# Retention, then a two-layer MLP, on one core: four plain fp32 units in place of eight, blocks 0 to 3 in another order, and two pairs at once in batch 1

## The chip, the cores and the metric

The kernel runs on one core of a Trainium2 chip. The time is in microseconds on the device, the median of five runs; a profile of one execution stands beside it. A core has five engines that each work through a queue of instructions in order: PE (TensorE, matmul; its weight loads are shown apart as PEld), DVE (VectorE), ACT (ScalarE), POOL (GpSimd) and SP (SyncE, which here only issues DMAs). Semaphores tie them together. DMAs issued by SP and by ACT run on the same 16 DMA engines. SBUF is the working memory, PSUM the eight banks that matmuls write to.

## What is computed

```python
# q, k, v: (8, 8, 576, 64)  batch, head, position, dim
scores = q @ k.T / sqrt(64)
ret = (scores * Dmat[h]) @ v         # Dmat[h][i, j] = gamma[h] ** (i - j) for i >= j, else 0
x = ret.transpose(0, 2, 1, 3).reshape(4608, 512)
h = x @ w_in                         # (4608, 512) @ (512, 2048)
g = max(h, 0) + alpha * min(h, 0)
out = g @ w_out                      # (4608, 2048) @ (2048, 512), float32
```

The weights arrive as float64 and are turned into float32 on the chip.

## The kernel before

**Blocks, units, cells.** The 4608 rows of x are cut into 18 blocks of 256 tokens, the 2048 hidden columns into 8 units of 256. A cell is one unit of one block: first matmuls (x block times two 128-column strips of w_in), activation, second matmuls into accumulators. A list `order` (lines 869 to 874) says in which order blocks are visited and which units each visit does; a visit that does not finish a block stores its partial sum to memory (`o_kept`) and a later visit of that block loads it again and adds (`has`). Units 0 to 3 are done for all blocks first, because only four units' weights fit in SBUF (`wsl`, slots s, i for unit s and piece i); units 4 to 7 follow, and their weights are loaded back from `w32`, where they were kept after conversion. There are 144 cells.

**Plain and split.** A split cell (`unit`, line 1004, and `second`, line 1053) works in a faster number format with three matmuls per product: x, the weights and g are each cut into three words by ACT, POOL and DVE (`split_x` L906 to L925, `split_w` L677 to L683, `split_g` L1028 to L1037). A plain cell (`unit_plain` L940, `second_plain` L970) uses float32 matmuls on unsplit x and weights and needs no split. The first eight cells are plain: block 0 with units 0 and 1, block 1 with units 0 to 3, block 0 with units 2 and 3. Then blocks 2 to 13 follow with units 0 to 3 each, and so on. A split cell's second matmuls come two cells later (`LAG`).

**Weights.** Each unit has four pieces of 128 x 512 words. `weights(n)` converts the next n pieces: `convert` loads the float64 words (a "raw", 512 KB) into some free room, and ACT (L629, L631), DVE (L639, L641, L650) and POOL (L653) make float32 of it in a "home". The 16 pieces of units 0 to 3 are converted in the opening, with homes in lx0, lx1 and g0, g1, which are free then; the raws go through lx1, w0x and op. DVE's steps use PSUM bank psa1 as a scratch. `split_w(i)` cuts a converted piece into its slot w. The other 16 pieces are converted during the first pass, one each three cells from cell 10 (`ahead`).

**Attention.** Batch 0 is done in three parts (`part_*`, `last_part`; rooms in the weight slots that are still empty) with all heads together. Batches 1 to 7 go by pairs of heads, numbered 4 to 31: `load_kq` and `load_v` load, `operands(n)` scales q on POOL (L719), transposes k and q on DVE (L726) and scales k on ACT (L731); `joint(n)` issues the value matmuls of pair n - 1 (L747) and the score and state matmuls of pair n (L785, L793, L802), then masks the scores into `at` and chains the states through `su` (ACT L844, L854; DVE L849, L857, L860), whose result goes by DMA into `vn` for the value matmuls. kx, qx, at and su exist once, kT, qT, kn and vn twice. The scores and states of every pair use banks psa0 and psa1, the values psh0 and psh1, which the first matmuls of cells use too. For pairs 4 to 7 (`FIRST`) the q and kn loads are issued by ACT and the masks done by ACT and POOL (L816, L822); for the others by SP and DVE (L831). `joint_(x)` does a joint, the operands of the next pair and the loads of the one after. Block 2 needs the values of pairs 4 to 7 and so do blocks 3 and 4 (in part); blocks 0 and 1 need batch 0.

**Order.** The program is written as a list of operations (`do`, `dma`) with engine, assumed cost, what they read and write. `plan()` (line 224) then places them on the engines by list scheduling: at each step the operation that can start first goes next, ties by a due time. The due time comes from PE's own order in the list: each PE operation is wanted at the sum of the costs of those before it, and every other operation is due early enough for its users. The instructions are issued in the order that comes out. `dma` (line 218) issues a load or store on SP or ACT with no limit on how many are under way. Lines 1109 to 1176 list the opening, lines 1178 to 1224 the main loop from cell 8; `todo` says at which cell each later joint comes.

## Time and profile before

| what | value |
|---|---|
| median of 5 runs | 986.21 us (982.54 to 991.15) |
| profiled execution, time | 986.21 us |
| profiled execution, span from first to last instruction | 984.2 us |
| mean granted clock of PE | 0.981 |
| PE busy | 942.4 us, 96% of the span |
| PEld busy | 826.1 us |
| DVE, ACT, POOL busy | 614.7, 583.3, 636.5 us |
| moved by DMA | 134.93 MB, 137 GB/s on average |
| L1004, first matmuls of split cells | 3264 matmuls, 420.2 us |
| L1053, second matmuls of split cells | 1632 matmuls, 403.1 us |
| L940 and L970, plain cells | 128 and 64 matmuls |

The span is cut into 40 slices in the profile; a digit there is a share of a slice in tenths. Busy time of PE is from modelled ends of pipelined matmuls, so a full PE can still lose a little. The granted clock is that of TensorE: where it is 0.5, matmuls take twice as long. A wait in the trace is put down to what released it last.

### The profile page before, as it was taken

The page shows a single profiled execution, that of the slowest core. Times are in us where ns is not written, and L with a number is a line of the kernel's source. Part 1 is how long each engine was busy: PE and PEld are TensorE (multiplying, and loading weights), DVE is VectorE, ACT ScalarE, POOL GpSimd, SP SyncE. Part 2 cuts the span into 40 slices and gives each one's busy share as a digit, 9 for nine tenths or more (in the row PEclk, how much of TensorE's full clock was granted, in tenths as well). Part 3 has the DMA queues.
Part 4 walks back from the last instruction along what each step waited for, and adds up shares of the span by engine and source line. Part 5 has one row for each costly group of instructions (what it writes and reads, how often), then busy time and mean ns, then how long its engine had stood idle before and what let it go on. Part 6 is the DMA issues. An engine that isn't in the chain of part 4 may idle for free.

```text
span 984.2 us, 22760 instructions
## 1 busy us (share of the span) xinstructions
PE 942.4 (96%) x8713; PEld 826.1 (84%) x8713; DVE 614.7 (62%) x1294; ACT 583.2 (59%) x1313; POOL 636.5 (65%) x515
## 2 busy tenths in 40 slices
PE   5897989999999999999999999999999999999998
PEld 4664668889889888887889899999999999999996
DVE  6667766777667787776566777564454444544444
ACT  4464456757556657574686766665555555555542
POOL 4667665767766758574697999665556556565553
PEclk9798889999999999999999999999999999999999
DMA  9988788788675888787442544242212222221111
GB/s 231 225 176 192 157 209 166 183 180 200 172 149 140 196 174 209 162 217 171 164 141 98 176 135 162 79 156 88 65 65 77 79 81 65 66 82 47 43 45 64
DMA packets 255052, 134.93 MB, mean 137 GB/s; under 512 B 218448, under 2 KB 218464, under 8 KB 254944
## 3 DMA queue, kind: packets, MB, share of 16 engines
q1 hardware_dynamic: 238624, 130.59, 51.7%
q10 hardware_dynamic: 16320, 2.89, 1.8%
q8 instruction: 68, 1.11, 0.5%
q14 instruction: 40, 0.33, 0.1%
HBM read 82.19 MB, written 35.65 MB: 120 GB/s over the span
## 4 chain that ended last, share of the span: by engine, by line
PE 84%; DVE 4%; DMA 4%; SPq 3%; ACT 2%; issue 2%; POOL 1%; ACTq 0%; POOLq 0%; DVEq 0%
PE psh L1004 36%; PE pso L1053 34%; PE psh L940 4%; PE psh L747 3%; SPq L220 3%; PE pso L970 3%; PE psa L793 1%; PE psa L802 1%; DMA w<-in_q_dram 1%; DMA vn<-su 1%; DMA kn<-in_k_dram 1%; DVE at L831 1%; PE psh L785 1%; DMA op<-in_moe_w_out_dram 0%; DMA qx<-in_q_dram 0%
## 5 line engine op out<-in xcount | busy, mean ns | idle before, releaser
L1004 PEld LDWEIGHTS psh<-lx,w 128*128 128x128 f32 x3264 | 411.6, 192 | 15.0 <-DVE ga L1019 2.6
L1004 PE MATMUL psh<-lx,w 128*128 128x256 f32 x3264 | 420.2, 285 | 2.0 <-DVE ga L1019 1.2
L1053 PE MATMUL pso<-w,g 128*128 128x512 f32 x1632 | 403.1, 394 | 0.8 <-POOL g L1035 0.3
L1053 PEld LDWEIGHTS pso<-w,g 128*128 128x128 f32 x1632 | 297.2, 189 | 58.2 <-POOL g L1035 1.2
L1032 POOL TENSOR_TENSOR g<-ga,g 128x512 fp32r<-128x512 f32 x136 | 179.1, 1317 | 253.0 <-ACT g L1028 252.6
L1013 DVE SCALAR_TENSOR_TENSOR ga<-psh,gt 128x256 f32<-128x256 f32 x272 | 114.6, 422 | 184.7 <-ACT gt L1012 175.9
L1035 POOL TENSOR_TENSOR g<-g 128x512 fp32r<-128x512 f32 x136 | 177.3, 1303 | 11.7 <-ACT g L1030 1.4
L1019 DVE SCALAR_TENSOR_TENSOR ga<-psh,malpha,ga 128x256 f32<-128x256 f32 x272 | 130.8, 481 | 69.3 <-ACT psh L1016 67.5
L1016 ACT ACTIVATE psh<-ga 128x256 f32<-128x256 f32 x272 | 105.3, 388 | 92.0 <-DVE ga L1013 91.2
L1028 ACT ACTIVATE g<-ga 128x512 fp32r<-128x512 f32 x136 | 85.9, 631 | 117.3 <-PE pso L1053 98.5
L1012 ACT COPY gt<-psh 128x256 f32<-128x256 f32 x272 | 100.9, 371 | 61.4 <-PE psh L1004 53.1
L923 POOL TENSOR_TENSOR lx<-lx 128x512 fp32r<-128x512 f32 x78 | 100.8, 1307 | 17.5 <-DVE lx L913 16.6
L1030 ACT ACTIVATE g<-ga 128x512 fp32r<-128x512 f32 x136 | 84.4, 621 | 0.0
L831 DVE SCALAR_TENSOR_TENSOR at<-psa,pf,mask 64x256 f32<-64x256 f32 x96 | 46.4, 483 | 17.5 <-PE psh L747 9.5
L906 ACT ACTIVATE lx<-x 128x512 fp32r<-128x512 f32 x78 | 47.1, 627 | 0.0
L719 POOL TENSOR_TENSOR qx<-qx,tabx 128x576 f32<-128x576 f32 x28 | 32.5, 1162 | 21.2 <-DMA qx<-in_q_dram 19.9
L747 PEld LDWEIGHTS psh<-at,vn 128*64 128x64 f32 x1008 | 33.0, 138 | 12.9 <-issue 7.2
L920 POOL TENSOR_TENSOR lx<-x,lx 128x512 fp32r<-128x512 f32 x30 | 38.2, 1292 | 3.5 <-ACT lx L918 3.4
L747 PE MATMUL psh<-at,vn 128*64 128x64 f32 x1008 | 38.4, 226 | 2.2 <-DVE ga L1019 1.6
L1071 DVE TENSOR_TENSOR op<-pso,op 128x512 f32<-128x512 f32 x46 | 31.5, 685 | 13.6 <-PE pso L1053 13.6
L940 PE MATMUL psh<-x,lx 128*128 128x256 f32 x96 | 30.0, 477 | 5.8 <-POOL lx L653 2.4
L731 ACT ACTIVATE kn<-kn,tabk 128x576 f32<-128x576 f32 x28 | 21.8, 777 | 22.1 <-DMA kn<-in_k_dram 19.2
(173 smaller groups left out, 863.2 us busy)
## 6 DMA issues: line engine op xcount, KB each, us to landing
ok<-o SPq DMA_DIRECT2D x48, 256.0 KB, 3.1
op<-ok SPq DMA_DIRECT2D x24, 512.0 KB, 4.0
x<-xk SPq DMA_DIRECT2D x23, 512.0 KB, 3.7
xk<-x SPq DMA_DIRECT2D x18, 512.0 KB, 3.6
out_dram<-o SPq DMA_DIRECT2D x36, 256.0 KB, 2.5
kx<-in_k_dram SPq DMA_DIRECT2D x112, 72.0 KB, 3.3
vn<-in_v_dram SPq DMA_DIRECT2D x56, 144.0 KB, 3.6
at<-qT SPq DMA_DIRECT2D x56, 144.0 KB, 3.2
```

The costliest lines, as they stand in the source:

```text
L747: nc.tensor.matmul(pv[i].get()[half(h2), (j - js[0]) * C:(j - js[0] + 1) * C], vns[n % 2][:, h2, j], mt.get()[:, h2, j], start=True, stop= ...
L923: do("POOL", 1.29, lambda c=c: nc.gpsimd.tensor_tensor(out=piece(to.get()[:, 2, c]), in0=to.get()[:, 0, c], in1=to.get()[:, 1, c], op=ALU. ...
L1004: nc.tensor.matmul(at(b), piece(w[:, l, c0:c0 + P]), piece(x.get()[:, l, cc]), start=(n == 0 and cc == 0), stop=(n > 0 and cc == NCC - 1), ...
L1012: do("ACT", 0.36, lambda t=t, at=at: nc.scalar.copy(t(), at(1)), [(ph, 1)], [(gt, f)])
L1013: do("DVE", 0.42, lambda t=t, g=g, at=at: nc.vector.scalar_tensor_tensor(out=g(), in0=at(0), scalar=ONE, in1=t(), op0=ALU.mult, op1=ALU.su ...
L1016: do("ACT", 0.39, lambda g=g, at=at: nc.scalar.activation(at(1), g(), ACTF.Relu, scale=-1.0), [(ga, f)], [(ph, 1)])
L1019: do("DVE", 0.48, lambda g=g, at=at, fc=fc: nc.vector.scalar_tensor_tensor(out=g(), in0=at(1), scalar=malpha[:, fc:fc + 1], in1=g(), op0=A ...
L1028: do("ACT", 0.64, lambda: nc.scalar.mul(piece(to.get()[:, 2]), ga.get(), BELOW), both, [(to, 2)])
L1030: do("ACT", 0.64, lambda: nc.scalar.mul(piece(to.get()[:, 0]), ga.get(), BELOW * 2.0 ** -12), both, [(to, 0)])
L1032: do("POOL", 1.29, lambda: nc.gpsimd.tensor_tensor(out=piece(to.get()[:, 1]), in0=ga.get(), in1=to.get()[:, 2], op=ALU.subtract), both + [ ...
L1035: do("POOL", 1.29, lambda: nc.gpsimd.tensor_tensor(out=piece(to.get()[:, 2]), in0=to.get()[:, 0], in1=to.get()[:, 1], op=ALU.subtract), [( ...
L1053: nc.tensor.matmul(a[2 * m + b].get(), piece(g.get()[:, l, f, m * P:(m + 1) * P]), piece(w_at[u, 2 + f].get()[:, l]), start=(cell["first"] ...
```

## The change

The opening and the plan are rewritten in these points:

1. **Four plain cells.** Only cells 0 to 3 are plain: blocks 0 and 1, each with units 0 and 1. The main loop starts at cell 4.
2. **Visit order.** Blocks 0 and 1 with units 0 and 1 (plain), block 2 with units 0 and 1, block 3 with units 0 to 3, then blocks 2, 1 and 0 with units 2 and 3, all split. From block 4, which is cell 16 in both kernels, the order is as before. There are 44 visits in place of 42, so two more partial sums are kept and added again. A visit whose block is the same as that of the visit before the last reuses its split x without loading or splitting it (visits 4, 21, 24 and 27).
3. **Two chains in batch 1.** Pairs 5 and 7 (`APART`) have their own kx, qx, at and su, in the room of lx0, and use banks pso2 and pso3 for scores and states. The plain cells' accumulators are pso0 and pso1 at every visit.
4. **Weights.** Pieces 0 to 7 get homes in lx1 and g0, with raws in lx0, x3, x4 and op. Pieces 8 to 15 are converted in the room they were loaded to (w3x, op), with no PSUM bank, and split from there. Eight pieces are split before cell 4; pieces 8 to 15 follow between the joints. The conversions of units 4 to 7 start at cell 18.
5. **Backward pass.** The due times come from a list scheduling of the same operations from the end backwards, all engines counted.
6. **Bytes in flight.** In the first 100 us of the plan a DMA on SP waits for an earlier one, so that no more than 1.31 MB, its own included, are under way.

```diff
     def dma(to, fro, size, r, w, eng="SP"):
-        queue = {"SP": nc.sync, "ACT": nc.scalar}[eng]
-        do(eng, 0.56, lambda: queue.dma_start(to(), fro()), r, w, late=size / RATE)
+        def f():
+            ins = {"SP": nc.sync, "ACT": nc.scalar}[eng].dma_start(to(), fro())
+            if now[0] < LIMITED:
+                ahead = size
+                for other, n in reversed(flight):
+                    if eng == "SP" and ahead >= IN_FLIGHT:
+                        tc.add_manual_dep(ins.ins, other.ins.name, mybir.DependencyInfo(
+                            mybir.DependencyClass.Sync, mybir.DependencyReason.DATA),
+                            reason="bytes in flight")
+                        break
+                    ahead += n
+                flight.append((ins, size))
+        do(eng, 0.56, f, r, w, late=size / RATE)
+
+    flight, now = [], [0.0]
+    LIMITED, IN_FLIGHT = 100.0, 5 << 18
...
-            due = [1e9] * len(ops)
-            for op in reversed(ops):
-                due[op.n] = min([want[op.n]] + [due[u.n] - wait(op, u) - op.cost - op.late
-                                                for u in users[op.n]])
...
+        for _ in ops:
+            pick = None
+            for e, queue in ready.items():
+                if queue:
+                    t0 = min(max(free[e], can[op.n]) for op in queue)
+                    op = max((op for op in queue if max(free[e], can[op.n]) <= t0 + 0.02),
+                             key=lambda op: op.n)
+                    t = max(free[e], can[op.n])
                     if pick is None or t < pick[0]:
                         pick = t, op
+            t, op = pick
+            ready[op.eng].remove(op)
+            free[op.eng] = t + op.cost
+            due[op.n] = -(t + op.cost)
+            for d in op.deps:
+                left[d.n] -= 1
+                can[d.n] = max(can[d.n], t + op.cost + wait(d, op) + d.late)
+                if not left[d.n]:
+                    ready[d.eng].append(d)
...
-    LAG, FIRST = 2, range(4, 8)
+    LAG, FIRST, APART = 2, range(4, 8), (5, 7)
...
+    def apart():
+        if not aside:
+            g = Gen(lxs[0])
+            aside.append(g)
+
+            def at(a, b):
+                return lambda: words_of(g)[:, a:b]
+            g.kx, g.qx, mt, su = at(0, S), at(S, 2 * S), at(2 * S, 4 * S), at(4 * S, 4 * S + 8 * D)
...
     def load_kq(n):
         b, c = pairs[n]
-        kx, qx, kn = Gen(kxs), Gen(qxs), Gen(kns[n % 2])
+        if n in APART:
+            kx, qx, kn = apart(), apart(), Gen(kns[n % 2])
+        else:
+            kx, qx, kn = Gen(kxs), Gen(qxs), Gen(kns[n % 2])
...
-        ps = [Gen(psa[p2]) for p2 in range(2)]
+        ps = [Gen(b) for b in ((pso[2], pso[3]) if n in APART else psa)]
...
-    order = [(0, (0, 1)), (1, (0, 1, 2, 3)), (0, (2, 3))]
-    order += [(kb, (0, 1, 2, 3)) for kb in range(2, 14)]
+    order = [(0, (0, 1)), (1, (0, 1)), (2, (0, 1)), (3, (0, 1, 2, 3)), (2, (2, 3)), (1, (2, 3)),
+             (0, (2, 3))]
+    order += [(kb, (0, 1, 2, 3)) for kb in range(4, 14)]
...
     def split_x(vis):
+        if vis["n"] > 3 and visits[vis["n"] - 2]["kb"] == vis["kb"]:
+            vis["x"] = visits[vis["n"] - 2]["x"]
+            return
...
-    raws = iter([((spare, 0), kTs[1]), ((spare, 1024), qTs[1]), ((spare, 2048), was)] +
-                3 * ([((wsl[0, i], 0), None) for i in range(4)] + [((op_, 0), was)]))
+    raws = iter([((spare, 0), kTs[1]), ((spare, 1024), qTs[1]), ((spare, 2048), was),
+                 ((xs[3], 0), kTs[1]), ((xs[4], 0), qTs[1]), ((op_, 0), was), ((xs[3], 0), kTs[1]),
+                 ((xs[4], 0), qTs[1])] + [((wsl[3, i], 0), None) for i in (0, 1, 2, 3, 1, 2, 3)] +
+                [((op_, 0), was)])
...
     part_states(1, bank)
     unit_plain(cells[1])
     load_part(2)
+    load_kq(NPAIR)
+    load_v(NPAIR)
     part_values(1, bank)
     part_carry(1)
     fetch_x(visits[1])
-    load_kq(NPAIR)
-    load_v(NPAIR)
     part_scale(2, 1)
     part_scale(2, 2)
     second_plain(cells[1])
-    unit_plain(cells[2])
     last_part()
     operands(NPAIR)
     load_kq(NPAIR + 1)
     load_v(NPAIR + 1)
-    weights(2)
+    joint_(4)
+    unit_plain(cells[2])
+    joint_(5)
+    for i in range(8):
+        split_w(i)
     second_plain(cells[2])
     unit_plain(cells[3])
...
     joint_(6)
     weights(2)
...
     joint_(7)
-    second_plain(cells[6])
-    unit_plain(cells[7])
+    second_plain(cells[3])
+    weights(2)
     joint_(8)
-    second_plain(cells[7])
-    for i in range(16):
+    for i in range(8, 12):
         split_w(i)
+    for i in range(12, 16):
+        weights(1)
+        if i > 12:
+            split_w(i - 1)
+    split_w(15)
 
-    todo = {}
-    at = 8
-    for b in range(2, B):
-        n = NS * sum(ready_kb[kb] == b - 1 for kb in range(2, 13)) or 6
+    todo = {4: [9], 7: [10], 10: [11], 12: [12]}
+    at = 16
+    for b in range(3, B):
+        n = NS * sum(ready_kb[kb] == b - 1 for kb in range(4, 13)) or 6
...
-    ahead = {10 + 3 * i: 1 for i in range(16)}
+    ahead = {18 + 14 * i // 5: 1 for i in range(16)}
...
-    for cell in cells[8:]:
+    for cell in cells[4:]:
...
     for op in best[1]:
+        now[0] = best[2][op.n]
         op.fn()
```

The lines left out of the diff rename keys and give `load_kq`, `operands`, `values` and `joint` the accessors for the second set of buffers, add the converted-in-place case to `convert`, and put the forward list scheduling, which is otherwise as before, one level out of a loop that ran once.

## The prediction

> **What bounds the kernel now.** I read the page's head and slices first, then the busy time by stage, then the chain of waits, once at the start and once at the end.
>
> ```profile
> span 984.2 us, 22760 instructions
> ...
> PE   5897989999999999999999999999999999999998
> ...
> PEclk9798889999999999999999999999999999999999
> DMA  9988788788675888787442544242212222221111
> ```
>
> A slice is 24.6 us. PE is full from slice 7 to the end, except for one 8 where attention runs out (about 450 to 490 us) and the drain. So time can only come out of the first six slices, out of PE's own work, or out of that one hole. In the early slices the granted clock is down too, and DMA is nearly full.
>
> ```profile
> 0.00:131.50 131.50, 102.28 (x1422) 71.51 (x1422) 93.26 (x195) 67.37 (x130) 82.08 (x85) 0.89 0.90 194
> ```
>
> ```profile
> 82.70:140.10 57.40, 44.51 (x526) 32.13 (x520) 40.87 (x76) 28.63 (x66) 39.52 (x37) 0.82 0.79 174
> ```
>
> The columns are the stretch, its length, busy us of PE, PEld, DVE, ACT and POOL, then granted clock, DMA share and GB/s. Up to the first split cell at 131.5 us PE does something for 102.3 us at a mean clock of 0.89. In the 57.4 us in which batch 1's pairs go through, PE is idle for 12.9 us.
>
> ```profile
> 66.69 0.62 PE psa L793 x32
> ...
> 69.69 3.45 PE psh L940 x16
> ...
> 73.41 3.63 PE pso L970 x8
> ...
> 81.87 0.87 PE psh L747 x24
> 82.76 0.37 ACT x L762
> ...
> 88.51 1.26 POOL g L653
> 89.77 0.04 issue
> 89.81 3.38 PE psh L940 x8
> ...
> 100.38 6.64 PE psh L940 x16
> ...
> 124.12 1.22 PE psh L747 x36
> ...
> 131.53 5.64 PE psh L1004 x24
> ```
>
> Start, length, what. A plain cell costs 3.45 + 3.63 = 7.08 us of PE (L940, L970). After a gap the same 16 matmuls take 6.64 us: half clock. Pair 4's scores (L793) start at 66.69, pair 7's values (L747) at 124.12: 57.4 us for four pairs, one at a time, with gaps of which 82.7 to 89.8 is the longest. The split of block 2 follows, and its first cell starts at 131.53, 6.2 us after those values end.
>
> ```profile
> 962.35 2.87 PE psh L1004 x24
> 965.22 2.75 PE pso L1053 x12
> ```
>
> A split cell costs 2.87 + 2.75 = 5.62 us, 1.46 less than a plain one.
>
> **Where the two kernels meet.** Cell 16, block 4 with unit 0, is the same cell in both, and from it on the same cells and pairs 13 to 31 follow. Before, the 24 L1004 matmuls at 184.98 are the second half of cell 15 and the first of cell 16, so cell 16 starts at 184.98 + 1.43 = 186.4. The change is worth what it moves this point, plus what the other due times do behind it. Before, split cells start at cell 8, at 131.5; after, at cell 4, at a time I call T. From there to cell 16 the kernel before takes 54.9 us for 8 cells and joints 9 to 12; after there are 4 more cells, 4 x 5.62 = 22.5 us. So the move is (T - 131.5) + 22.5 + c, where c is new PE waiting. T = 109 is the break-even.
>
> **T, step by step.** (1) Joint 4 waits for the last part of batch 0, which uses bank psa0 until 64.8. Its transposes run at 58.5, behind the 16 plain matmuls that the chain has at 53.94 to 57.46, though POOL's last scaling of that part (L393) ended at 52.6. The backward pass gives this chain an earlier due time than the plain cell, which is worth those 3.5 us; bounds 0, and 8 from the end of part 1's values (50.3). Joint 4 at 63.2. (2) A pair from scores to values, bare: scores and states 1.09 (0.62 + 0.47, L793 and L802), su copy 0.35, two L849 1.02, copy 0.21, L857 and L860 1.28, the su transfer 2.8, 1.22 of values: 8.0. Pair 4 took 15.2 (66.7 to 81.9), with conversions between its steps. I take 11, nearer the bare chain as half the conversions leave this stretch; bounds 8 and 15. (3) Pairs 5 and 7 get own kx, qx, mt and su and the banks pso2 and pso3, so the four run as two waves: 11 each, 3 for the second pair of the wave (masks on ACT and POOL are 1.9 and 3.1 a pair), and a turn of 4 between (the v load after values takes 3.5 to land, then states 0.47). 11 + 4 + 11 + 3 = 29. Values of pair 7 at 92.2, end at 93.4, and 6.2 for the split: **T = 99.6**, a move of -31.9 + 22.5 = **-9.4**.
>
> **Does DMA allow it?** Needed by T: parts 3.5 MB, twelve pieces 6.3, four pairs at 1.74 each 6.9 (five times 288 KB and 256 of su), loads of pairs 8 and 9 about 2, stores of x and o 2.1: 20.8 MB. At the 194 GB/s of that row it is 107 us, at the 231 of the first 25 us 90. T lies in the middle, so transfers are as much a limit as the chains. The limit of 1.31 MB in flight makes SP wait before issues up to a planned 100 us; behind it on SP all later loads and the at<-qT and vn<-su transfers queue. At 231 GB/s 1.31 MB is 5.7 us of work, and weight transfers already take 5 us to land, so I cost it at nothing; if its waits leave DMA empty for 0.5 us at some ten places it is 5 us.
>
> The Trainium skill, page "DMA: Bandwidth & Descriptors", section "Issuing engines are not separate DMA queues", says that queues share the 16 engines and that using several saves issue time only. By that rule the limit could not shorten the loads on ACT's queue by adding bandwidth; this trace has both queues full together but no row that tests it, and the sum takes no gain here either way.
>
> **c, the crowd in cells 4 to 15.** These 77.4 us now also hold x splits of blocks 1, 0 and 3 and the last pieces. POOL: 12 x 2.62 for g, 4 splits x 5.2, 4 x 1.16 for qx, pieces 12 to 15 at 2.75 (L653 1.34, L678 1.41): 68 us, 88%. DVE: 12 x 1.81, evacuations 11.1 (three visits now add to a kept o), 4 pairs x 6.33, 4 pieces x 2.98 (0.61, 0.55, 0.79 and 1.03 of L639 to L681): 70 us, 90%. Rows of full PE to hold this against:
>
> ```profile
> 200.00:250.00 50.00, 49.88 (x583) 44.89 (x582) 37.25 (x87) 33.78 (x80) 33.29 (x28) 1.00 0.86 202
> ...
> 550.00:600.00 50.00, 49.37 (x319) 44.84 (x318) 34.87 (x63) 33.91 (x76) 47.18 (x36) 1.00 0.49 154
> ```
>
> POOL at 94% left PE 98.7% busy; DVE at 75% cost nothing, and at 90% no full stretch shows it. If DVE can give 81% (20.2 of 25 us from 100 to 125), 70 us need 86, +9. If pieces 8 to 11 are late too, POOL needs 79/0.94 = 84, +6.6. I take **c = +3**, bounds 0 and 9, as POOL's row is the one with PE full. The cover is PE's own work; without it two more splits are 10 us.
>
> **The rest.** Three later visits (21, 24, 27) reuse their x split and one load each goes: POOL and ACT work under a full PE, 0. Two more visits store and reload o, 0 for the same reason. Eight pieces convert in place, where L639 and L641 take 0.61 and 0.55 against 0.69 and 0.70 through a bank: 0.23 each on DVE, off the path. The plain accumulators stay on pso0 and pso1: the next visit waits for two ACT copies of 0.6, long done, 0. The new due times reorder every engine. Behind cell 16 only the hole at 450 to 500 us can answer: 3.7 us idle and 3.4 us at half clock, 5.4 in all. Bounds -5.4 and +5.4; I take **-1.5**.
>
> **Sum:** -9.4 + 3 - 1.5 = -7.9; span 976.3 from 984.2. The profiled execution's time, 986.2, is the median of the runs shown, so the time is **978**.
>
> The clock speaks against fewer plain cells. The trace: 3.2 us lost at 100.4, 2.8 at 131.5, each after a gap. The Trainium skill, page "TensorE: Matmul & The Clock Gate", section "HAM oscillation", says idle gaps above about 3.4 us throw PE to half rate, and its section "What's actually happening" gives 3.4 us to warm up again, a loss of half that, an estimate of 1.7 a gap. Four plain cells cover less, so each of two wave gaps would cost 1.7 by the rule and 3 by the rows; in the sum above only the one ahead of T sits on the path, in 54.9 already.
>
> **Rivals.** (A) The pairs are paced by the engines and the transfers, not by the single buffers: DVE, POOL and DMA were 71, 69 and 79% busy from 82.7 to 140.1, and pairs came every 13 to 15 us. If two chains only interleave, at 12 us a pair with the lighter load, values of pair 7 start at 63.2 + 4 x 12 + 1 = 112, T = 119.6, the sum is +10.6 + 3 - 1.5: time **998**. It decides from T = 109, that is from a mean of some 9.6 us a pair. For it: DMA at 0.9 over this stage. Against: the longest gaps end on one pair's own chain. (B) Gain and crowd cancel: T = 102, c = 7, hole 0: -29.5 + 22.5 + 7 = 0: **986**. For it: DVE at 87%. Against: POOL at 94% with a full PE. (C) The bare chain: 8 us a pair, c = 0: T = 93.6, -15.4 - 1.5: **969**; DMA would need 20.8 MB in 94 us, 222 GB/s, which only the first 50 us exceed (231 and 227).
>
> **Chances.** Forecast 0.46 (own range 972 to 982), C 0.18, B 0.17, A 0.19. Faster by over 0.5% (about what a measurement here can tell from no change, 4.9 us): forecast and C, 0.64; same 0.17; slower 0.19. The range takes C's side down to 962 (with step 1's other end too) and A's up to 995, where pairs come every 11 to 12 us.
>
> **What would show it.** First L1004 matmul near 100 us; L793 groups in two couples; L747 of pair 7 near 92; PE idle under 25 us up to cell 16, near 177; four plain cells (64 L940 matmuls, not 128); no new wait in cells 4 to 15 over 2 us. Wrong, if the first split cell comes after 109, if PE waits on POOL L653/L678 or DVE L681 for unit 2 or 3, or if the stretch behind cell 16 takes other than 798 us by more than 5.

## The result, and the profile after

The kernel after takes 990.07 us (median of 53 runs, 986.35 to 993.91), the kernel before, run beside it, 987.82 us (95 runs, 980.57 to 993.53): a ratio of 1.002, 95% interval 1.0012 to 1.0028. The forecast was 978 and faster; the change costs about 2 us. The profiled executions, 989.2 against 984.2 us of span, lie 5.0 us apart, more than the medians do: that of after was 0.9 us above its kernel's median, that of before 1.6 below. The places below are read from these two.

The page of after, head and slices:

```profile
span 989.2 us, 22943 instructions
...
PE   4786699999999999999999999999999999999997
...
PEclk9998699999999999999999999999999999999999
DMA  9997888777775888778544444243222222221112
```

The hole that the kernel before had at 450 to 490 us is gone, and PE is full from slice 6 on, one slice earlier than before. But slices 4 and 5 now stand at 6, slice 5 at a clock of 0.6: in the opening PE stands more, not less.

The windows view of after: the stretch up to the first split cell, the one up to cell 16, the four pairs, and the old hole (columns as before: stretch, length, busy us of PE, PEld, DVE, ACT, POOL, clock, DMA share, GB/s):

```profile
0.00:112.50 112.50, 74.68 (x1326) 54.97 (x1326) 79.03 (x168) 57.32 (x112) 70.20 (x77) 0.88 0.93 193
112.50:190.40 77.90, 76.22 (x795) 68.24 (x793) 62.27 (x129) 55.01 (x128) 66.85 (x52) 0.97 0.84 204
...
59.50:105.00 45.50, 32.05 (x457) 21.58 (x456) 32.45 (x64) 22.62 (x50) 23.28 (x24) 0.83 0.83 176
450.00:500.00 50.00, 49.50 (x569) 42.90 (x561) 32.68 (x77) 32.83 (x80) 35.72 (x29) 1.00 0.62 178
```

While the four pairs go through (third row) no engine is busy for more than 71% (DVE, 32.45 of 45.5). The DMA engines are at 0.83. It is a stage of waits. In the old hole PE has 49.50 us where the kernel before had 46.26.

PE's timeline in after (start, length, what; in brackets the idle time before and who ended it):

```profile
59.49 0.70 PE L834 MATMUL psa<-qT,kT 64*64 64x64 f32 x32
...
72.52 0.69 PE L834 MATMUL pso<-qT,kT 64*64 64x64 f32 x32 [0.17 <-DVE qT L767]
73.14 0.34 PE L788 MATMUL psh<-at,vn 128*64 128x64 f32 x4
77.19 2.27 PE L788 MATMUL psh<-at,vn 128*64 128x64 f32 x32 [3.71 <-DMA vn<-su]
79.38 5.38 PE L989 MATMUL psh<-x,lx 128*128 128x256 f32 x16
84.69 0.92 PE L788 MATMUL psh<-lx,vn 128*64 128x64 f32 x24
...
88.92 0.70 PE L843 MATMUL psa<-vn,kn 64*64 64x64 f32 x32
...
97.01 2.46 PE L788 MATMUL psh<-at,vn 128*64 128x64 f32 x32 [2.35 <-DMA vn<-su]
...
101.12 0.48 PE L788 MATMUL psh<-lx,vn 128*64 128x64 f32 x4
...
111.42 1.13 PE L834 MATMUL psa<-qT,kT 64*64 64x64 f32 x32 [3.11 <-DVE su L905]
112.48 2.93 PE L1053 MATMUL psh<-lx,w 128*128 128x256 f32 x12
```

L834 are scores (L793 before), L843 states (L802), L788 values (L747), L989 plain first matmuls (L940), L1053 first matmuls of split cells (L1004). Joint 4's scores start at 59.5, values of pair 4 at 73.1 (most of them at 77.2, finished at 79.4), of pair 5 at 84.7, states of pair 6 at 88.9, most of its values at 97.0, pair 7's values at 101.1, the first split cell at 112.5. Before, the same way from joint 4's scores took 57.4 us to pair 7's values; after it takes 41.6, and 29 had been forecast.

The account, by the prediction's own points: T is 112.5, 19.0 earlier. From T to cell 16 it is 77.9 us (190.4 - 112.5), where 54.9 and four more cells make 77.4, so c is +0.5. Behind cell 16 it is 798.8 us against 797.8. That is -19.0 + 22.5 + 0.5 + 1.0 = +5.0.

### The profile page after: what moved, and what is told of

The parts are those of the page before. It is cut to its first block, busy times and chain, and to the rows that moved or that the text cites. A ratio compares the mean times of both kernels' runs of the same rounds, so it can differ in the third digit from the quotient of the medians.

```text
span 989.2 us, 22943 instructions
## 1 busy us (share of the span) xinstructions
PE 937.6 (95%) x8761; PEld 828.9 (84%) x8761; DVE 632.7 (64%) x1306; ACT 589.7 (60%) x1329; POOL 651.3 (66%) x525
## 4 chain that ended last, share of the span: by engine, by line
PE 79%; DMA 8%; DVE 4%; ACT 3%; SPq 2%; issue 2%; POOL 1%; ACTq 0%; POOLq 0%; DVEq 0%
PE psh L1053 37%; PE pso L1102 35%; PE psh L788 3%; SPq L220 2%; DMA kn<-in_k_dram 2%; PE psh L989 1%; PE psa L834 1%; PE psa L843 1%; DMA vn<-su 1%; DMA w<-in_q_dram 1%; DMA w<-in_moe_w_out_dram 1%; DMA lx<-in_q_dram 1%; DMA op<-in_moe_w_out_dram 1%; DMA op<-in_moe_w_in_dram 1%; DMA kx<-in_k_dram 1%
## 5 line engine op out<-in xcount | busy, mean ns | idle before, releaser
L1053 PEld LDWEIGHTS psh<-lx,w 128*128 128x128 f32 x3360 | 423.3, 192 | 21.0 <-DVE ga L1068 8.4
L1053 PE MATMUL psh<-lx,w 128*128 128x256 f32 x3360 | 433.8, 285 | 5.7 <-DVE ga L1068 4.9
L1102 PE MATMUL pso<-w,g 128*128 128x512 f32 x1680 | 413.8, 393 | 0.6 <-POOL g L1084 0.3
L1102 PEld LDWEIGHTS pso<-w,g 128*128 128x128 f32 x1680 | 305.1, 189 | 58.5 <-POOL g L1084 0.7
L1081 POOL TENSOR_TENSOR g<-ga,g 128x512 fp32r<-128x512 f32 x140 | 186.0, 1329 | 226.7 <-ACT g L1077 226.4
L1084 POOL TENSOR_TENSOR g<-g 128x512 fp32r<-128x512 f32 x140 | 183.0, 1307 | 11.3 <-ACT g L1079 0.9
L1068 DVE SCALAR_TENSOR_TENSOR ga<-psh,malpha,ga 128x256 f32<-128x256 f32 x280 | 134.0, 480 | 65.1 <-ACT psh L1065 63.7
L1077 ACT ACTIVATE g<-ga 128x512 fp32r<-128x512 f32 x140 | 88.4, 631 | 121.5 <-PE pso L1102 108.7
L1079 ACT ACTIVATE g<-ga 128x512 fp32r<-128x512 f32 x140 | 86.7, 620 | 0.0
L877 DVE SCALAR_TENSOR_TENSOR at<-psa,pf,mask 64x256 f32<-64x256 f32 x96 | 46.3, 482 | 11.9 <-PE psh L788 3.4
L788 PEld LDWEIGHTS psh<-at,vn 128*64 128x64 f32 x936 | 32.9, 143 | 17.7 <-issue 8.0
L969 POOL TENSOR_TENSOR lx<-x,lx 128x512 fp32r<-128x512 f32 x34 | 44.5, 1308 | 4.8 <-DMA at<-qT 3.4
L788 PE MATMUL psh<-at,vn 128*64 128x64 f32 x936 | 38.4, 232 | 8.8 <-DMA vn<-su 7.2
L1120 DVE TENSOR_TENSOR op<-pso,op 128x512 f32<-128x512 f32 x52 | 35.6, 685 | 14.3 <-PE pso L1102 14.3
L760 POOL TENSOR_TENSOR qx<-qx,tabx 128x576 f32<-128x576 f32 x26 | 30.2, 1162 | 15.0 <-DMA qx<-in_q_dram 11.5
L1125 DVE SCALAR_TENSOR_TENSOR o<-pso,op 128x512 f32<-128x512 f32 x52 | 35.7, 687 | 1.1
L803 ACT COPY x<-psh 128x256 f32<-128x256 f32 (+3 forms) x84 | 23.4, 319 | 20.6 <-PE psh L788 12.7
## 6 DMA issues: line engine op xcount, KB each, us to landing
ok<-o SPq DMA_DIRECT2D x52, 256.0 KB, 3.2
out_dram<-o SPq DMA_DIRECT2D x36, 256.0 KB, 4.1
```

Of the source, the lines that this page charges most:

```text
L788: nc.tensor.matmul(pv[i].get()[half(h2), (j - js[0]) * C:(j - js[0] + 1) * C], vns[n % 2][:, h2, j], mt.mt()[:, h2, j], start=True, stop=True)
L1053: nc.tensor.matmul(at(b), piece(w[:, l, c0:c0 + P]), piece(x.get()[:, l, cc]), start=(n == 0 and cc == 0), stop=(n > 0 and cc == NCC - 1), ...
L1068: do("DVE", 0.48, lambda g=g, at=at, fc=fc: nc.vector.scalar_tensor_tensor(out=g(), in0=at(1), scalar=malpha[:, fc:fc + 1], in1=g(), op0=A ...
L1077: do("ACT", 0.64, lambda: nc.scalar.mul(piece(to.get()[:, 2]), ga.get(), BELOW), both, [(to, 2)])
L1079: do("ACT", 0.64, lambda: nc.scalar.mul(piece(to.get()[:, 0]), ga.get(), BELOW * 2.0 ** -12), both, [(to, 0)])
L1081: do("POOL", 1.29, lambda: nc.gpsimd.tensor_tensor(out=piece(to.get()[:, 1]), in0=ga.get(), in1=to.get()[:, 2], op=ALU.subtract), both + [ ...
```

## The experiments

Fifteen kernels; each ratio is to the kernel before, run beside it. That kernel's own median was between 987.82 and 990.25 us in the several rounds, so compare the ratios and not the medians. "First split cell", "cell 16" and the stretch behind it are from each one's profiled execution, which lies between 2.1 us below (b_kn_sp) and 4.3 us above (a_eight_more) its kernel's median.

How far such readings scatter can be read from five of the kernels. In the traces of after, a_no_limit, a_eight_more, a_eight_big and a_reuse4 every engine has the same instructions in the same order up to the first split cell. It starts at 112.5, 113.0, 113.9, 114.4 and 114.4 us, and cell 16 at 190.3 to 192.3. So a difference of 2 us in these two columns shows nothing by itself, and the stretch behind cell 16 scatters more.

| kernel | median, us | ratio, 95% interval | first split cell | cell 16 | behind it |
|---|---|---|---|---|---|
| before | 987.82 | 1 | 131.5 | 186.4 | 797.8 |
| after | 990.07 | 1.002 (1.0012 to 1.0028) | 112.5 | 190.4 | 798.8 |
| a_no_limit | 989.98 | 1.001 (0.9993 to 1.0026) | 113.0 | 190.3 | 796.9 |
| a_old_due | 1011.67 | 1.0229 (1.0209 to 1.025) | 110.9 | 199.8 | 811.2 |
| a_one_chain | 1000.89 | 1.0114 (1.0093 to 1.0136) | 126.8 | 203.3 | 796.2 |
| a_visits | 992.04 | 1.0032 (1.0012 to 1.0052) | 112.7 | 196.3 | 795.8 |
| a_kn_sp | 987.39 | 0.9989 (0.9974 to 1.0005) | 112.0 | 190.9 | 797.3 |
| a_unit3_early | 986.33 | 0.9976 (0.9961 to 0.9991) | 111.6 | 188.5 | 797.7 |
| a_both | 989.2 | 0.999 (0.9972 to 1.0009) | 115.0 | 192.5 | 798.5 |
| a_eight_more | 992.47 | 1.0024 (1.0006 to 1.0042) | 113.9 | 192.1 | 803.0 |
| a_eight_big | 988.24 | 0.9982 (0.9963 to 1.0001) | 114.4 | 191.7 | 797.2 |
| a_no_unit2 | 985.87 | 0.9957 (0.9942 to 0.9972) | 109.1 | 188.9 | 795.2 |
| a_reuse4 | 988.07 | 0.9984 (0.997 to 0.9997) | 114.4 | 192.3 | 792.7 |
| a_reuse4_unit3 | 981.76 | 0.9927 (0.9899 to 0.9956) | 111.0 | 187.8 | 796.1 |
| b_backward | 981.28 | 0.9923 (0.9905 to 0.994) | 126.7 | 186.9 | 792.7 |
| b_ahead_late | 982.44 | 0.994 (0.9919 to 0.9961) | 127.3 | 188.3 | 791.2 |
| b_kn_sp | 982.85 | 0.9934 (0.9907 to 0.996) | 130.9 | 186.2 | 792.6 |

### The parts of the change, one by one

**The limit off** (a_no_limit):

```diff
-    LIMITED, IN_FLIGHT = 100.0, 5 << 18
+    LIMITED, IN_FLIGHT = 0.0, 5 << 18
```

> The changed kernel without the limit on bytes in flight, nothing else undone. Theory L (the limit's waits are not in the plan and hold SP back in front of transfers that batch 1's chains need: pair 4's state transfer was issued 8.1 us after its data were ready, 4.3 us of it an SP wait on another transfer): that transfer goes out by about 69.5 us instead of 73.8, the first split cell starts 4 us or more earlier than 112.5 (108 or less), and the time falls by 4 us or more, to 986 or less. Rival D (the transfers are slow because the DMA engines are full; the limit only moves the queue from the engines to SP): the state transfer lands no earlier than 76 us, first split cell within 2 us of 112.5, time within 2 us of 990.

No difference. The longest of SP's waits from 45 to 112 us stays. After first, then a_no_limit (line, what it waited for: us in total, times, longest):

```profile
SPq L220 <- DMA kn<-in_k_dram: 4.3, 1, 4.3
```

```profile
SPq L220 <- DMA kn<-in_k_dram: 4.8, 1, 4.8
```

The wait belongs to the transfer vn<-su, which needs no kn. In both programs the DMAs of SP and ACT take eight completion semaphores in turn (the 698 DMAs in after's trace use each of them 87 or 88 times), and a DMA waits for the one that had its semaphore eight DMAs earlier. So only some eight are under way anyhow, with or without the limit. That this turn is the reason is read from the programs' instructions; a version with more semaphores wasn't tried.

**The old due times** (a_old_due), and **the backward pass alone in the kernel before** (b_backward). The first replaces the second block by the first, the other kernel does the reverse:

```diff
-            if op.eng == "PE":
-                want[op.n] = at
-                at += op.cost
...
-            due[op.n] = min([want[op.n]] + [due[u.n] - wait(op, u) - op.cost - op.late
+            due[op.n] = -(t + op.cost)
```

> The changed kernel with the due times of the kernel before (PE's order in the list) in place of the backward pass. Theory B (the backward pass puts raws, conversions and a plain cell ahead of batch 1's chains in the in-order queues of SP, ACT and PE, and costs a few us behind cell 16 as well): faster than the changed kernel by 2 us or more, first split cell before 110. Rival (the backward pass is worth something, as it was forecast): slower by 2 us or more, in the opening or in the hole near 480 us. No difference over 2 us: it is worth nothing.

> The kernel before with the backward pass alone. Forecast: -1.5 us, bounds -5.4 and +5.4, in the hole at 450 to 490 us. Theory B (it costs): slower than before by 2 us or more, in the opening. If the time is within 2 us of 987.8 the backward pass cannot explain why the gain failed to come.

The pass is worth some 21 us in the kernel after (ratios 1.0229 and 1.002) and 7 in the kernel before, which it makes faster than both. In a_old_due the first split cell is not later (110.9): cell 16 comes 9.4 us later, and the stretch behind it is 12.4 longer. In b_backward cell 16 stays where it was, and all of the gain lies behind it. The windows view from 450 to 500 us, before, then b_backward:

```profile
450.00:500.00 50.00, 46.26 (x473) 39.11 (x472) 27.62 (x65) 30.37 (x73) 26.70 (x22) 0.97 0.55 165
```

```profile
450.00:500.00 50.00, 49.20 (x514) 43.09 (x513) 35.40 (x79) 33.43 (x81) 35.75 (x28) 1.00 0.54 171
```

The hole is filled: DVE, ACT and POOL are busier there too (35.40 us of DVE for 27.62). From cell 52 to cell 54 the kernel before takes 26.2 us, b_backward 18.6.

**One chain of pairs** (a_one_chain):

```diff
-    LAG, FIRST, APART = 2, range(4, 8), (5, 7)
+    LAG, FIRST, APART = 2, range(4, 8), ()
```

> The changed kernel with pairs 5 and 7 on the common kx, qx, at, su and banks psa, so one chain at a time as before. If two chains bring what they were taken to (29 us instead of 57 for four pairs, of which 41.5 were measured): the first split cell comes 10 us or more later than 112.5 and the time is 1000 or more. Rival (the pairs are paced by SP's queue and the transfers, not by the single buffers): within 3 us of 990.

The second chain brings 14.3 us at the first split cell (12.4 against the latest of the five profiles with after's opening) and some 9 in time (ratios 1.0114 and 1.002). With the backward pass, eight plain cells and one chain the ratio is 0.9923; with four plain cells, the new order and layout and one chain 1.0114. So that part costs some 19 us, and the second chain wins back 9 of them. (The limit is in the second of these and not in the first; it costs nothing.)

**Block 2 in one visit** (a_visits):

```diff
-    order = [(0, (0, 1)), (1, (0, 1)), (2, (0, 1)), (3, (0, 1, 2, 3)), (2, (2, 3)), (1, (2, 3)),
+    order = [(0, (0, 1)), (1, (0, 1)), (2, (0, 1, 2, 3)), (3, (0, 1, 2, 3)), (1, (2, 3)),
```

> The changed kernel with block 2 done in one visit of four units, so 43 visits in place of 44, one partial sum less kept and added, no reuse of block 2's split x; units 2 and 3 are then needed at cells 6 and 7 and not 8 and 9. If the change's visit order only costs its extra work under a full PE: within 1.5 us of 990. If unit 2's and 3's weights are late (they are split up to about 125 us, cell 6 starts at 126.7): slower by 2 us or more. If the extra sums crowd DVE and cost as in the c of the forecast: faster by 2 us or more.

Cell 16 comes 5.9 us later (4 to 6 against the five profiles). In its trace PE waits 3.8 us for DVE's emptying of banks (L1068), which stands behind conversions and splits of unit 2 in the chain (L664, L672, L703), and after that wait a second split cell runs at half clock too (24 first matmuls in 5.29 us). So with four plain cells the new visit order, which asks for unit 2 later, is worth those 4 to 6 us up to cell 16. In time it doesn't show: the ratios are 1.0032 and 1.002, with overlapping intervals, and the stretch behind cell 16 is 3.0 shorter in this profile.

**Later conversions in b_backward** (b_ahead_late):

```diff
-    ahead = {10 + 3 * i: 1 for i in range(16)}
+    ahead = {18 + 14 * i // 5: 1 for i in range(16)}
```

> The kernel before with the backward pass, and the conversions of units 4 to 7 at the cells where the changed kernel has them (18 to 60, not 10 to 55). Behind cell 16 the changed kernel takes 798.8 us, this one with the old conversion cells 792.7, for the same cells. Theory A (the later, denser conversions cost these 6 us): the stretch behind cell 16 grows by 4 us or more and the time rises from 981.3 to 985 or more. Rival (they cost nothing, and the stretch is longer for what the opening leaves behind, or for the order the plan lands on): within 1.5 us of 981.3.

The edit moves conversions in the list, but the plan comes out as it was: in the traces of b_backward and b_ahead_late every engine has the same instructions in the same order. So this is b_backward once more, and shows only how far one program's numbers scatter (ratios 0.9923 and 0.994, first split cell 126.7 and 127.3). Whether the later conversions cost something in after, it can't say.

### Why the pairs take 41.6 us and not 29

The chain of waits in after, from joint 4's scores on (start, length, what):

```profile
59.56 0.63 PE psa L834 x32
...
62.91 0.72 POOL at L868
63.63 0.41 SPq L220
...
65.05 6.23 DMA w<-in_moe_w_out_dram
71.28 0.02 issue
71.30 0.61 ACT w L654
71.91 0.05 issue
71.96 1.85 ACT w L656 x3
73.83 3.23 DMA vn<-su
...
77.19 2.27 PE psh L788 x32
79.45 5.31 PE psh L989 x16
84.76 0.85 PE psh L788 x24
```

Pair 4's states are ready at 65.75 (end of its DVE L905), but their transfer is issued at 73.83. In between SP issues four q loads of pair 8, and then waits for kn loads that ACT issues. ACT's queue shows why those are late:

```profile
63.99 0.21 ACT L899 COPY su<-psa 128x64 f32<-128x64 f32 x1 [0.20 <-DVE psa L894]
67.90 0.66 ACT L654 ACTIVATE w<-w 128x512 f32<-128x512 f32 x1 [3.71 <-DMA w<-in_moe_w_in_dram]
67.93 0.64 ACTq L220 DMA_DIRECT2D kn<-in_k_dram  x1
```

ACT stands for 3.71 us on raw weights, and the kn loads stand behind that conversion. Then values of pair 5 (84.7) stand behind a plain cell (79.4 to 84.8, most of it at half clock). These were the two waits to take away.

**kn loads of pairs 6 and 7 on SP's queue** (a_kn_sp), **the last plain cell ahead of pair 5 in the list** (a_unit3_early), and **both** (a_both):

```diff
-                [(kn, h2)], "ACT" if n in FIRST else "SP")
+                [(kn, h2)], "ACT" if n in (4, 5) else "SP")
...
+    second_plain(cells[2])
+    unit_plain(cells[3])
     joint_(5)
...
-    second_plain(cells[2])
-    unit_plain(cells[3])
     joint_(6)
```

> The changed kernel with the four kn loads of pairs 6 and 7 issued by SP, where ACT issued them between 67.9 and 71.9 us, behind conversions that waited for raw weights. Removing the byte limit changed nothing, so pair 4's state transfer waits for something else: the program's instructions show one of eight completion semaphores, handed out in turn to the DMAs of both queues, so an issue on SP waits for the DMA eight before it, and those were ACT's late kn loads. Theory S: pair 4's state transfer goes out at 70 us or earlier instead of 73.8, the first split cell starts 2 us or more before 112.5, and the time falls by 2 us or more. Rival D (the DMA engines are full, 0.91 of 16 from 50 to 75 us, and whichever queue issues, the bytes land no sooner): state transfer lands after 75.5, first split cell and time within 2 us of the changed kernel's 112.5 and 990.

> The changed kernel with the second matmuls of cell 2 and the first of cell 3 listed ahead of joint 5, so that they take bank psh0 before pair 4's values and not between those of pairs 4 and 5. There they ran at half clock from 79.4 to 84.7 us with pair 5's values waiting behind them. Theory P (plain cells, listed between the values of a wave, hold the chains on the banks they share): pair 5's values follow pair 4's within 2 us, the first split cell starts 4 us or more before 112.5, and the time falls by 4 us or more, to 986. Rival D or S (transfers set the pace): pair 5's values come earlier but the first split cell moves by less than 2 us, as the loads of the next pairs are late anyway.

> The kernel after with both repairs of the opening at once: kn loads of pairs 6 and 7 on SP's queue, and the last plain cell ahead of pair 5 in the list. If the two waits (vn<-su of pair 4 behind the kn loads, values of pair 5 behind the plain cell) are separate links of one chain, the gains of 2.7 and 3.7 us add: 983 to 985, first split cell near 110 or earlier. If another limit stands right behind them, it is 986 to 988 and the first split cell stays at 111 to 112.

The way of the four pairs can be cut into the steps that the prediction added up, by the starts of PE's groups: from pair 4's scores to its values (the group of 32 or 36), to pair 6's states (the turn), to pair 6's values (again the large group), to pair 7's values.

| kernel | pair 4's scores at | to its values | to pair 6's states | to its values | to pair 7's values | sum |
|---|---|---|---|---|---|---|
| forecast | 63.2 | 11 | 4 | 11 | 3 | 29 |
| after | 59.5 | 17.7 | 11.7 | 8.1 | 4.1 | 41.6 |
| the five with after's opening | 59.5 to 61.8 | 16.4 to 18.6 | 10.9 to 11.9 | 7.8 to 8.1 | 4.1 to 4.7 | 39.5 to 42.7 |
| a_kn_sp | 61.8 | 14.3 | 10.1 | 10.7 | 3.6 | 38.7 |
| a_unit3_early | 60.5 | 17.2 | 7.0 | 9.4 | 7.1 | 40.7 |
| a_both | 61.6 | 16.4 | 9.7 | 10.5 | 4.3 | 40.8 |
| a_no_unit2 (below) | 61.2 | 14.5 | 9.4 | 8.9 | 3.2 | 36.0 |

Each edit shortens the step that it was made for, and later steps take most of it back. With kn on SP, vn<-su goes out 11.5 us after pair 4's scores, not 14.3, and that step is 3.4 shorter; pair 6's step is longer by 2.6. With the plain cell moved, the turn is 4.7 shorter, but values of pair 5 start at 86.0, later than without the edit, and the last two steps are 4.3 longer. Together they don't add: values of pair 5 wait until 89.1. The first split cell moves by -0.5, -0.9 and +2.5 us, hardly more than the scatter. The times are better than that: ratios of 0.9989, 0.9976 and 0.999, where after has 1.002, so some 3 to 4 us faster each (a_kn_sp and a_both only just clear of after's interval). For a_unit3_early this shows at cell 16, at 188.5 (187.8 in a_reuse4_unit3, which has the same opening) for 190.3 to 192.3; its time fell to the 986 that theory P gave, but not by the way that it gave.

**Eight more loads on SP, small and large** (a_eight_more, a_eight_big):

```diff
+    idle = Gen(slot(attn, "idle", [P, 32]))
...
+        if 6 <= n < 10:
+            for i in range(2):
+                dma(lambda i=i: idle.get()[0:16, 16 * i:16 * i + 16],
+                    lambda: moe_alpha.rearrange("(t p) -> t p", p=P)[:, 0:16], 1024, (),
+                    [(idle, i)])
```

In a_eight_big `idle` is 128 x 2 x 256 words and each load fills a half from `w_in`.

> The kernel after with 8 loads of 1 KB more on SP, two with each of pairs 6 to 9, whose data nothing reads. Theory Q, the opening is paced by the number of DMAs (SP issues one in 0.6 us, in order, and each waits for the one eight before it): 8 x 0.6 = 4.8 us, the first split cell at 116 to 118 and the time 3 to 5 us up. Theory D, the opening is paced by bytes: 8 KB are nothing, the first split cell stays within 1.5 us of 112.5 and the time within 2 us of 990. Theory E, by the engines' chains: as D.

> The same 8 more loads on SP with 131 KB each in place of 1 KB, 1.05 MB in all. Theory Q: as the kernel with the 1 KB loads, first split cell at 116 to 118. Theory D: 1.05 MB at the 190 GB/s of the opening are 5.5 us, first split cell near 118 while the 1 KB loads leave it at 112.5. Theory E, neither bytes nor issues but the engines' chains pace the opening: it stays within 1.5 us of 112.5 in both.

The loads did not come where they were wanted: the plan put all eight behind the first split cell. The issues of `idle` in a_eight_more, then in a_eight_big (number; shortest, median and longest issue in ns; first and last start in us):

```profile
L220 SPq DMA_DIRECT2D idle<-in_moe_alpha_dram x8: 370/496/1382, 174.0 to 205.5; - x8
```

```profile
L220 SPq DMA_DIRECT2D idle<-in_moe_w_in_dram x8: 333/463/659, 173.9 to 208.1; - x8
```

Up to there both are the program of after, so the first split cell at 113.9 and 114.4 is scatter and decides nothing between Q, D and E: whether the number or the bytes of the DMAs pace the opening is not tested. What the profiles show fits a limit of the transfers as well: up to the first split cell all of these kernels, before and after too, move 187 to 198 GB/s at a DMA share of 0.90 to 0.97, wherever between 109 and 131.5 us that cell stands. (a_eight_more keeps after's order to the end; its 803.0 us behind cell 16 are from a profile 4.3 us above its median. In a_eight_big the order differs from 213 us on, and the time is lower, 0.9982 against 1.0024 with intervals apart.)

**No load and no conversion of pieces 8 to 11** (a_no_unit2):

```diff
             at = npiece[0]
+            if 8 <= at < 12:
+                npiece[0] += 1
+                next(raws)
+                continue
...
-            key = plain[at]
+            key = plain[at] if u != 2 else (w_at[0, i], 0)
```

> The kernel after without the loads and conversions of pieces 8 to 11 (unit 2): their splits are made of unit 0's split instead, so unit 2's part of the result is not the reference's. This takes 2.1 MB of loads, and per piece 1.35 us of ACT (L654, L656), 2.1 of DVE (L664, L666, L672) and 1.28 of POOL (L675) out of the opening. Theory W, conversions that stand in the engines' queues between the pairs' steps are why the four pairs take 41.5 us from joint 4's scores to pair 7's values and not 29: with half of those between 59 and 112 us gone, values of pair 7 move to 93 to 96 and the first split cell to 100 to 105. Theory E, the pairs' own steps, their transfers and the plain cells between them take that long: the first split cell stays at 110 or later. Theory D, bytes: 2.1 MB at 190 GB/s are 11 us, the first split cell near 101 as in W, but then the 1.05 MB of the earlier run should have cost 5.5 us and it cost 1.9.

In between. From joint 4's scores (61.2) to pair 7's values (97.1) it is 36.0 us, 3.5 to 6.7 less than in the five profiles with after's opening; so the loads and conversions of these pieces account for that much of the 12.6 us that the forecast lacked. Which of the two it is, the run doesn't say: both were left out, and the plan filled their room with other work (POOL is busy for 28.25 us from 59.5 to 105.0, where after has 23.28; up to the first split cell 193 GB/s are moved, as in after). The rest belongs to what remains beside and in the pairs (other conversions, plain cells, masks, transfers), which these runs don't divide further. T moves by 3.4 (5.3 against the latest of the five), the time by 6 (ratios 0.9957 and 1.002). What stands ahead of the first split cell then (PE's timeline of a_no_unit2):

```profile
77.94 4.88 PE L991 MATMUL psh<-x,lx 128*128 128x256 f32 x16
...
102.74 1.48 PE L845 MATMUL psa<-vn,kn 64*64 64x64 f32 x32
108.06 1.13 PE L836 MATMUL psa<-qT,kT 64*64 64x64 f32 x32 [3.84 <-DVE su L907]
109.13 3.96 PE L1055 MATMUL psh<-lx,w 128*128 128x256 f32 x24
```

Joint 9's scores, which the split cell doesn't need, stand before it in PE's queue and wait 3.84 us for DVE's chain of pair 8; in after the same wait is 3.11 us. Without these scores ahead of it the split cell would still have waited for POOL's last step of its split x, which ends at 108.81 here and at 111.28 in after: at most 0.3 and 1.2 us were to be had.

### Where the gain of the backward pass went

PE's waits from 190 to 600 us: b_backward, then after, then a_reuse4.

```profile
PE psh L762 <- DVE ga L1034: 1.0, 2, 0.7
PE psh L1019 <- DVE ga L1034: 0.7, 1, 0.7
```

```profile
PE psh L1053 <- DVE ga L1068: 4.2, 8, 0.8
PE psh L788 <- DMA vn<-su: 1.2, 1, 1.2
```

```profile
PE psh L1053 <- DVE ga L1068: 2.2, 4, 0.7
PE psh L788 <- DMA vn<-su: 1.0, 1, 1.0
```

First matmuls of split cells wait for DVE to empty their bank, eight times in after. Counted from cell 16, after falls 5.9 us behind b_backward by cell 76 and 0.3 after that. By cells (us between their first matmuls, one profile each):

| cells | before | b_backward | b_ahead_late | after | a_no_limit | a_eight_more | a_reuse4 | a_unit3_early | a_reuse4_unit3 |
|---|---|---|---|---|---|---|---|---|---|
| 16 to 52 | 249.6 | 252.8 | 251.6 | 256.0 | 254.5 | 258.3 | 252.1 | 255.0 | 255.5 |
| 52 to 76 | 155.4 | 146.9 | 146.5 | 149.6 | 149.6 | 150.0 | 147.7 | 149.6 | 147.7 |
| 76 to the end | 393.0 | 392.9 | 393.0 | 393.2 | 392.9 | 394.7 | 392.9 | 393.3 | 392.9 |

The middle row hardly scatters, and the gain stands there: 8.5 us in the kernel before, of which after keeps 5.8. The first row scatters: after, a_no_limit, a_eight_more and a_reuse4 have one order up to cell 52, but for a few small loads, and take 252.1 to 258.3 us. What after loses there against b_backward, one profile of each can't tell.

**The split x kept at visit 4 alone** (a_reuse4), and the same **with the plain cell moved** (a_reuse4_unit3):

```diff
-        if vis["n"] > 3 and visits[vis["n"] - 2]["kb"] == vis["kb"]:
+        if vis["n"] == 4 and visits[vis["n"] - 2]["kb"] == vis["kb"]:
...
-            if vis["n"] > 3 and visits[vis["n"] - 2]["kb"] == kb:
+            if vis["n"] == 4 and visits[vis["n"] - 2]["kb"] == kb:
```

> The kernel after with the split x of the block before kept at visit 4 alone (visits 21, 24 and 27 load and split again, as in the kernel before). The stretch behind cell 16 takes 798.8 us after and 792.7 in the kernel before with the backward pass alone. Theory R, the kept splits hold a buffer too long and cost those 5 to 6 us: the stretch comes to about 793 and the time to 984 or 985. Theory O, the loss is the order that the plan lands on, block by block: the stretch stays at 796 to 800 and the time within 2 us of 990.

> The kernel after with two edits that moved it alone: split x kept at visit 4 only (988.1 alone, stretch behind cell 16 of 792.7), and the last plain cell ahead of pair 5 in the list (986.3 alone, cell 16 at 188.5). If the two are independent, cell 16 stands at 188.5 to 190 and the stretch behind it takes 793: time 983 to 985, below the kernel before. If each only redraws the planner's order and the gains are luck of the order, it is 986 to 991 and the stretch 796 to 800.

In a_reuse4 the stretch is 792.7 us, that of b_backward to a tenth, but by luck: every engine has after's order up to 490 us, so its later cell 16 (by 1.9 us) and its shorter way from there to cell 52 (by 3.9) are scatter. What the edit does stands at cells 66 to 76, where visits 21 and 24 used the kept x: 57.2 us for 59.2. With the plain cell moved it is 57.2 for 59.2 again. In time the gain is 3.6 us (ratios 1.002 and 0.9984) in the one opening and 4.9 (0.9976 and 0.9927) in the other, with intervals apart both times. So giving up the late reuses gains, about alike in both openings: 2 us where the traces can place it, 4 to 5 in time. a_reuse4_unit3, at 981.76 us, is clearly faster than the kernel before and as fast as b_backward. Why a kept x makes DVE later stays open.

**kn on SP in b_backward** (b_kn_sp): the edit of a_kn_sp.

> The kernel before with the backward pass, and the kn loads of pairs 6 and 7 on SP's queue. If the ACT queue behind its conversions holds back the loads there too, the first split cell comes 1 to 2 us earlier than 126.7 and the time is 979 to 981; if not, it stays within 1.5 us of 981.3.

The time is the same within the intervals, and the first split cell comes at 130.9, some 4 us later than in the two profiles of b_backward's order. Moving the kn loads gains nothing in this opening.

## Why the prediction was wrong

**The failed step is (3), "the four run as two waves ... 11 + 4 + 11 + 3 = 29".** From joint 4's scores to pair 7's values it took 41.6 us. In the prediction's own terms that is 17.7 + 11.7 + 8.1 + 4.1. The second wave held (12.2 for 14). The whole excess is in pair 4's way from scores to values, 17.7 for 11 and outside the bounds of 8 and 15, and in the turn, 11.7 for 4. The 11 was a bare chain of 8 with 3 us for other work; the turn was one v load with nothing ahead of it. In the trace other work stands in both: four q loads on SP ahead of su's transfer, kn loads behind conversions on ACT, a plain cell of 5.4 us on PE in the turn. The waves show in the states (pairs 4 to 7 at 60.0, 62.5, 88.9 and 91.6), but not, as forecast, in the scores (59.5, 53.1, 66.9 and 72.5).

Of the cause a part is shown: without the loads and conversions of four pieces the way is 3.5 to 6.7 us shorter. Taking away a single wait shortened its own step by 3 to 5 us, and later steps took most of that back. That waits in in-order queues make up the rest is read from the traces and not shown; that the transfers set the pace would fit as well.

**Steps (1) and the rest of (3).** Joint 4 came at 59.5, not 63.2, better than forecast and inside the bounds (0 to 8 earlier). The reason given, the backward pass, is not it in this kernel: in a_old_due, without the pass, pair 4's scores come at 58.0. Pair 7's values took 4.1 us in place of 1.2, and from their end to the split cell 7.2 in place of 6.2. Together: -3.7 + 12.6 + 3.0 + 1.0 = 12.9, all of T's miss (112.5 for 99.6).

**Break-even.** The prediction put it at T = 109. T came at 112.5 and the kernel became a little slower, as that says. So rival A decides rightly on which side the time falls, with pairs at 10.4 us each (41.6 / 4) and not 12. Of its reason, pairs paced by busy engines and transfers, the first half doesn't hold, as no engine was over 71% busy; the second, with the DMA engines at 83% over these 45.5 us, is not tested. The row that the prediction read as the stretch of the pairs before, 82.7 to 140.1, was not theirs: from 66.7 to 124.1 PE is idle for 9.4 us and not 12.9, DVE is 76% busy and not 71, and the DMA share is 0.82 and not 0.79.

**DMA.** 193 GB/s up to T, 21.7 MB, against the 20.8 estimated: the amount was right. The prediction's own figure for these bytes at the rate of the opening, 107 us, was nearer to T than the 99.6 of the chains, which lay between it and the 90 at the rate of the first 25 us. Whether the share of 0.93 is a limit stays open, as both runs that were to test it have their loads behind T. The limit in flight at 0 was right; the worry of 5 us at ten places did not come.

**c** was put at +3 and is +0.5. The crowd on DVE was over-sized: 62.27 us in 77.9, 80%, where 70 us and 90% had been counted. POOL has 66.85 (68 counted), and PE waited for it hardly at all.

**The rest** was put at -1.5 and is +1.0. The mechanism was right: the hole is closed, 3.2 us of PE won at 450 to 500. Alone, the backward pass brings 5.1 behind cell 16 in its profile, near the bound of 5.4 that the prediction gave it. In after, cells 52 to 76 are 5.8 shorter than before. Two things stand against that. The late reuses of x cost 2.0 at cells 66 to 76, where the prediction had put 0, as work hidden under a full PE. And cells 16 to 52 took 6.4 more than in the one profile of before, in a stretch where four profiles of one order lie some 6 apart.

**The sum:** forecast -31.9 + 22.5 + 3 - 1.5 = -7.9, measured -19.0 + 22.5 + 0.5 + 1.0 = +5.0 in the profiles; 12.9 of difference, T's 12.9, with c and the rest cancelling. By the medians the change costs 2.3 us and not 5.0, so some 3 us of this sum are scatter of the two profiled executions. A gain was to be had in the part of the change that the prediction gave 1.5 us: the due times.

## What to carry to other kernels

Before buying overlap with extra work (here four more cells, 22.5 us), price the shortened chain with what stands in each in-order queue between its steps, not from its bare durations; pair 4 took 17.7 us where its bare chain is 8. A change of many parts should be run part by part: here one part gains 7 us alone, and the others give it back. When a wait is taken away and nothing moves, look at once for the wait behind it. Where a list scheduler draws the order, look up in the trace where an edit went: here eight loads meant for the opening came 60 us behind it, and one edit changed no engine's order. And compare stages with a second profile of the same instructions beside them; here such profiles put the first split cell up to 2 us apart.

## What the hardware showed that was not expected

- **Half clock.** The split cell that starts T does so at half clock, and stays there for some 4.4 us (a clock of 0.62 in the third row is half clock for 1.9 of its 2.5 us). The windows view of after, around the first split cell:

```profile
105.00:112.50 7.50, 2.90 (x71) 2.31 (x67) 3.39 (x8) 5.71 (x13) 6.24 (x5) 0.50 0.93 278
112.50:115.00 2.50, 2.50 (x15) 2.50 (x13) 2.28 (x2) 0.72 (x2) 2.42 (x3) 0.50 0.92 225
115.00:117.50 2.50, 2.50 (x18) 2.37 (x17) 2.46 (x3) 0.87 (x2) 2.42 (x3) 0.62 1.05 220
117.50:120.00 2.50, 1.72 (x61) 1.44 (x62) 1.41 (x4) 2.02 (x6) 0.91 (x1) 1.00 0.57 90
```

  Its 24 first matmuls take 5.06 us, 2.87 at full clock: 2.2 lost. The page "TensorE: Matmul & The Clock Gate" of the Trainium skill, section "What's actually happening", puts the change to the full clock after about 3.4 us of sustained work; an estimate from that is 1.7 us lost, half of it. For this cell the measurement, 4.4 and 2.2, is the one to use.

- **Issue time.** A DMA takes SP about 0.6 us to issue (1.11 for the two halves of vn<-su at 73.83), 76 issues and 47 us from 45 to 112. Whether that paces the opening is not tested.

- **DMAs in flight.** The limit of 1.31 MB changed nothing (989.98 against 990.07 us). As the programs' instructions read, the eight semaphores that the DMAs of both queues take in turn hold issues back in any case, 4.3 us for vn<-su of pair 4.

- **Scatter of one program.** From cell 16 to 52 four profiles of the same order took 252.1 to 258.3 us. From cell 76 to the end, with PE full, eight of the nine profiles in the table agree within 0.4 us (392.9 to 393.3; a_eight_more has 394.7).
